# Loading the first layer's bias rows in the weight queue and transposing them by themselves

## The chip, the cores and the metric

The kernel runs on one core of a Trainium2 chip. Time is the device time of one execution in microseconds (us), and lower is better. A core has a matrix engine (PE; its weight loads are shown as PEld), a vector engine (DVE), an activation engine (ACT), a general engine (POOL) and a queue engine (SP) that only issues transfers. Each engine runs its own instructions in a fixed order and waits on semaphores for the others. Transfers between main memory and the on-chip memory run on 16 DMA engines, and they are issued from the instruction streams of SP, ACT and POOL.

## The reference

The input `x` has 2048 positions of 640 values. Two branches are computed from it and mixed by a gate per position:

```python
g = sigmoid((x * gate_w).sum(-1))                      # one gate per position
# branch a: a diagonal state space layer with 640 complex states
Lam_bar = exp(exp(log_dt) * Lam);  B_bar = ((Lam_bar - 1) / Lam)[:, None] * Bmat
h[t] = Lam_bar * h[t-1] + B_bar @ x[t]
a = 2 * real(h @ Cmat.T) + x * Dskip
# branch b: two dense layers, 640 -> 1728 -> 640
b = gelu(x @ w1 + b1) @ w2 + b2
out = g * a + (1 - g) * b
```

The change concerns `b1`, the 1728 biases of the first dense layer. The activation engine needs them as columns (one value per partition), and main memory holds them in one row.

## The kernel before, in words

The positions are worked on in four blocks of 512 (`q`), and within them in 16 chunks of 128 (`c`). For each block PE computes the first dense layer (`m1`: 14 column tiles `jf` of 128, the last one 64 wide, each a sum over five contraction slices `k` of 128) and the projection into the states (`bproj`). ACT applies the GELU with the bias column (`ge`) or copies the projection out (`u`). DVE runs the state recurrence (`pre`, `scan`, `post`, two halves of 256 positions per block) and leaves the states in `H`. For each chunk PE then computes the second dense layer (`m2`, L776 and L777) and the projection out of the states (`cproj`, L802, which reads the transposed matrix `CT`). DVE adds the parts up and SP stores them.

The order of the work is made by a planner when the kernel is built (`Sched.order`). Every operation is declared with its engine, an estimated duration, a latency after it, the keys that it reads and writes, and a priority (a smaller number goes first). The planner always takes the engine that is free earliest and gives it, among the operations whose inputs are there by the estimates, the one of smallest priority. The result is a fixed order for each engine. The chip keeps that order, whatever the real times are.

Dependencies follow the order of declaration (`Prog.op`). An operation that writes a key waits for the last writer that was declared before it and for all readers of that writer's data. PSUM banks are such keys, `("bank", n)`.

The start of the kernel is what the change touches. These are its parts, with the lines of the profile:

- **SP** issues, by priority: the first half of x's first block (`x0_0`, 0), the W1 slices for the first six column tiles (`w1_0` 2, `w1_1` 3), the second half (`x0_1`, 3.5), `w1_2` 4, `w1_3` 5, `w1_4` 6, the rest of W1 (`w1_r`, 6.5), then DMA transposes of B, of x's second block, W2, the transposes of the rest of x, and at last the ten transposes that make `CT` (all issues L330, the transposing ones L337).
- **ACT** issues six small loads into one tile `rows`: five rows each for the real part, the imaginary part and the step of the states, 13 rows of `b1`, and the last 64 values of `b1` twice, into both halves of the last row. Then it loads its first function table.
- **PE** transposes the first half of x (`tp0..`, L426), and starts the first layer of block 0 slice by slice over six banks (`m1_first`, L637). The slices are taken as (0, first half of the positions), (1, first), (2, first), (0, second), (1, second), (2, second), and then slices 3 and 4 over all 512 positions. The second half of x is transposed in between: `tp1` for k = 0, 1, 2 in bank 6 (six transposes) and for k = 3, 4 in bank 7 (four transposes).
- **The columns**: one transpose on PE (`cols`, L400, priority 6.2) turns all 29 rows into columns in bank 7. DVE copies them out (`cols1`, L405) to `cols`, of which `lcol` is the part of the states and `b1col` the part of the biases.
- **DVE** copies the transposes of x to `xT` (`tpe..`, L435) and computes tables from `lcol`: `ang` (L461, L462), `psi0`, `psi1`, `psi2` (L476 to L490), `atab` (L579 and L581), then `small` and the large tables. By priority the copies of x go before all of them, and `atab` (-946) comes after `psi0` to `psi2` (-949) and after `small` (-948) where these can run.
- **Bank 7** is used in the order of declaration: `cols`, `cols1`, then `tp1` for k = 3, 4 and its copy `tpe13`, and later a bank of `m1`.

Of the kernel before, what the change touches and what calls it, by code (L numbers as in the profile page):

```python
# [8 lines left out]
FP32 = mybir.dt.float32  # L9
BF16 = mybir.dt.bfloat16  # L10
# [137 lines left out]
class Prog:  # L148
# [8 lines left out]
    def op(self, name, eng, dur, reads, writes, fn, prio=None, lat=0.0, after=()):  # L157
        deps = {}
        for k in reads:
            for w in self.last_w.get(k, ()):  # L160
                deps[w.idx] = w
        for k in writes:
            for w in self.last_w.get(k, ()):
                deps[w.idx] = w
            for r in self.last_r.get(k, ()):
                deps[r.idx] = r
        for a in after:
            deps[a.idx] = a
        deps = list(deps.values())
        E = self.E  # L170

        def run(eg, deps=deps, eng=eng, fn=fn):
            E.wait(eng, *[d.done for d in deps])
            return fn()

        it = self.sch.add(name, eng, dur, deps, run, prio=prio, lat=lat)
        for k in writes:
            self.last_w[k] = [it]
            self.last_r[k] = []
        for k in reads:  # L180
            self.last_r.setdefault(k, []).append(it)
        return it


def bass_gated_mix__ssm_conv_s5__dense_activation_gelu__prompt_kernel(
# [20 lines left out]
    F = B_w1.shape[1]  # L206
    assert S % 512 == 0 and D % 128 == 0 and P == D
    KD = D // 128
    KP = P // 128
# [4 lines left out]
    NF = (F + 127) // 128  # L214
    FL = F - (NF - 1) * 128
# [10 lines left out]
    with ExitStack() as es, nc.Block() as block:  # L226

        def SB(name, shape, dt):
            return es.enter_context(nc.sbuf_tensor(name, list(shape), dt))
# [8 lines left out]
        GlL = [SB(f"GlL_{i}", [65, 512], BF16) for i in range(3)]  # L238
        dsk = SB("dsk", [128, D], BF16)
        gwb = SB("gwb", [128, D], BF16)  # L240
        NR = 3 * KP + NF
        rows = SB("rows", [NR, 128], BF16)
        cols = SB("cols", [128, NR], FP32)
        lcol = cols[:, 0:3 * KP].rearrange("p (a k) -> p a k", a=3)
        b1col = cols[:, 3 * KP:NR]
        dtb = SB("dtb", [128, KP], BF16)
        acol = SB("acol", [128, KP], FP32)
        thcol = SB("thcol", [128, KP], FP32)
# [5 lines left out]
        ident = SB("ident", [128, 128], BF16)  # L254
# [51 lines left out]
        op = pr.op  # L306

        def inc(eng, ins):
            return E.inc(eng, ins, eng + "_s")

        def dma_inc(eng, ins, sem):
            SEM(sem)
            E.count.setdefault(sem, 0)
            ins.then_inc(sems[sem], 16)
            E.count[sem] += 16
            return (sem, E.count[sem])
# [11 lines left out]
        def load(name, eng, sem, dst, src, writes, prio, dur=0.5, lat=2.5, reads=(), **kw):  # L328
            def fn():
                return dma_inc(eng, engines[eng].dma_start(dst, src), sem)  # L330
            return op(name, eng, dur, reads, writes, fn, prio=prio, lat=lat)
# [17 lines left out]
        NW = 6  # L349
# [5 lines left out]
        nmain = (NF - 1) * 128  # L355

        for i, (nm, src) in enumerate((("lre", A_Lambda_re), ("lim", A_Lambda_im), ("ldt", A_log_dt))):
            load(nm, "act", "l_" + nm, rows[i * KP:(i + 1) * KP, :], src.rearrange("(k p) -> k p", p=128), [("rows", i)], prio=-100 + i, dur=0.45)
        load("b1a", "act", "l_b1a", rows[3 * KP:NR - 1, :], B_b1[0:nmain].rearrange("(j p) -> j p", p=128), ["b1a"], prio=-97, dur=0.4, lat=2.5)
        for h in range(2):  # L360
            load(f"b1b{h}", "act", f"l_b1b{h}", rows[NR - 1:NR, h * 64:h * 64 + FL], B_b1[nmain:F].rearrange("(j p) -> j p", j=1), [("b1b", h)],
                 prio=-96 + h, dur=0.4, lat=2.5)


        def f_iota():
# [31 lines left out]
        psC = PS[7][:, :].bitcast(BF16)  # L397

        def f_cols():
            return inc("pe", nc.tensor.transpose(psC[:, 0:NR], rows[:, :], ident[0:NR, 0:NR]))  # L400

        op("cols", "pe", 0.2, [("rows", 0), ("rows", 1), ("rows", 2), "b1a", ("b1b", 0), ("b1b", 1), "ident"], [("bank", 7)], f_cols, prio=NW + 0.2)

        def f_cols1():
            return inc("dve", nc.vector.tensor_copy(out=cols[:, :], in_=psC[:, 0:NR]))  # L405

        op("cols1", "dve", 0.2, [("bank", 7)], ["lcol", "b1col"], f_cols1, prio=-3000)


        def filler(name, n, prio, deps):  # L410
# [552 lines left out]
```

## Time and profile before

| | us |
|---|---|
| median of 6 runs (range) | 217.96 (217.69 to 218.3) |
| the profiled execution | 217.87 |
| its span, first to last instruction | 216.0 |
| PE busy | 211.9 (98%) |
| DVE busy | 191.8 (89%) |
| ACT busy | 99.5 (46%) |
| DMA engines' mean share, 5.5 to 11 us | 1.01 |
| granted PE clock in the whole span | 1.00 |

The span is what the profile shows from the first to the last instruction. The time of the same execution is 1.87 us longer. An engine's idle time before an instruction is written in brackets behind the instruction with what ended it; "SPq" and "ACTq" are instructions by which an engine issues a transfer. A matmul's bar includes its way through the array, so bars of consecutive matmuls overlap, and the distance from start to start says what each costs.

### The profile page before, as it was taken

To read this page: it belongs to the slowest core of one execution; us is meant where nothing else is said; L and a number is where in the kernel's file an instruction comes from. 1 tells how busy PE (TensorE), PEld (TensorE's weight loads), DVE (VectorE), ACT (ScalarE), POOL (GpSimd) and SP (SyncE) were. 2 spreads that over 40 slices of the span, in tenths; PEclk is the share of its full clock that TensorE was granted. 3 is DMA by queue.
4 is the path that set the end of the run, shared out by engine and by line. 5 is a ranking of instruction groups with operands and counts; after the bars stand their busy time and mean duration, and the time that the engine had idled before them with its cause. 6 is when DMAs were issued, how large, how long until landed. Compare 5 with 4: busy or idle time off the path is not lost.

```text
span 216.0 us, 3326 instructions
## 1 busy us (share of the span) xinstructions
PE 211.9 (98%) x1305; PEld 124.9 (58%) x1305; DVE 191.8 (89%) x269; ACT 99.5 (46%) x169; POOL 4.6 (2%) x13
## 2 busy tenths in 40 slices
PE   8999999999999999999999999999999999999995
PEld 3744444444567776444457777544447777777774
DVE  5699999999999999999996999599999999989513
ACT  2497556675433324556662322556662224233220
POOL 1010030000000100000000010000000000000000
PEclk9999999999999999999999999999999999999999
DMA  6995569997810040000000014000000001000001
GB/s 164 356 161 108 121 151 287 281 183 130 129 37 30 30 155 0 30 0 0 3 0 0 33 35 148 33 0 0 0 3 0 0 30 33 30 30 33 30 30 33
DMA packets 28202, 15.46 MB, mean 72 GB/s; under 512 B 22044, under 2 KB 27740, under 8 KB 28188
## 3 DMA queue, kind: packets, MB, share of 16 engines
q1 hardware_dynamic: 27568, 12.95, 25.6%
q0 software_dynamic: 560, 2.30, 3.6%
q8 instruction: 11, 0.18, 0.3%
q14 instruction: 3, 0.02, 0.0%
q10 hardware_dynamic: 60, 0.01, 0.0%
HBM read 7.38 MB, written 2.62 MB: 46 GB/s over the span
## 4 chain that ended last, share of the span: by engine, by line
PE 70%; SPq 26%; DMA 1%; issue 1%; DVE 0%
PE ps L776 25%; SPq L337 24%; PE ps L802 20%; PE ps L656 13%; PE ps L701 10%; SPq L330 2%; PE ps L777 2%; DMA CT<-in_A_C_im_dram 1%; PE ps L677 1%; DVE osb L835 0%
## 5 line engine op out<-in xcount | busy, mean ns | idle before, releaser
L776 PE MATMUL ps<-W2sb,Gl 128*128 128x320 bf16 x416 | 61.4, 299 | 0.0
L656 PE MATMUL ps<-xT,W1sb 128*128 128x512 bf16 x230 | 50.3, 379 | 0.0
L776 PEld LDWEIGHTS ps<-W2sb,Gl 128*128 128x128 bf16 x416 | 40.5, 98 | 16.6 <-issue 0.4
L802 PE MATMUL ps<-CT,H 128*128 128x320 bf16 (+2 forms) x330 | 46.1, 295 | 0.4 <-DMA CT<-in_A_C_im_dram 0.4
L741 DVE TENSOR_TENSOR_SCAN W<-atab,V 128x1280 bf16<-128x1280 f32 x16 | 44.3, 2812 | 0.3
L701 PE MATMUL ps<-xT,BT 128*128 128x512 bf16 x200 | 43.8, 379 | 0.0
L664 ACT ACTIVATE Gl<-ps,cols 128x512 bf16<-128x512 f32 x46 | 31.4, 690 | 16.7 <-PE ps L656 16.6
L802 PEld LDWEIGHTS ps<-CT,H 128*128 128x128 bf16 x330 | 31.7, 98 | 12.6 <-DMA CT<-in_A_C_im_dram 0.7
L656 PEld LDWEIGHTS ps<-xT,W1sb 128*128 128x128 bf16 x230 | 22.5, 98 | 27.2
L784 ACT ACTIVATE E<-ps,g1col 128x320 bf16<-128x320 f32 x32 | 16.9, 527 | 43.1 <-PE ps L777 43.1
L701 PEld LDWEIGHTS ps<-xT,BT 128*128 128x128 bf16 x200 | 19.5, 98 | 23.5 <-issue 0.4
L710 ACT ACTIVATE U<-ps 128x512 bf16<-128x512 f32 x40 | 23.9, 597 | 18.3 <-PE ps L701 18.3
L813 ACT ACTIVATE E<-ps,gcol 128x320 bf16<-128x320 f32 x30 | 15.8, 527 | 25.4 <-PE ps L802 25.4
L502 DVE TENSOR_TENSOR osb<-xg,E 128x640 bf16<-128x640 bf16 x15 | 7.3, 487 | 8.5 <-ACT E L813 7.4
L821 DVE SCALAR_TENSOR_TENSOR xg<-xn,gcol,dsk 128x640 bf16<-128x640 bf16 x16 | 13.9, 883 | 0.4
L613 DVE SCALAR_TENSOR_TENSOR scr<-xn,gwb 128x640 bf16<-128x640 bf16 x16 | 13.2, 822 | 0.4
L502 DVE TENSOR_TENSOR H<-H,V 128x1280 bf16<-128x1280 bf16 x16 | 12.5, 822 | 0.3
L502 DVE TENSOR_TENSOR V<-V,W 128x1280 bf16<-128x1280 bf16 x16 | 12.5, 822 | 0.3
L502 DVE TENSOR_TENSOR V<-mr,U 128x2560 bf16<-128x2560 bf16 x8 | 11.9, 1489 | 0.5 <-DVE s L502 0.3
L502 DVE TENSOR_TENSOR H<-c,W 128x2560 bf16<-128x2560 bf16 x8 | 11.9, 1488 | 0.1
L502 DVE TENSOR_TENSOR V<-s,W 128x2560 bf16<-128x2560 bf16 x8 | 11.9, 1485 | 0.0
L502 DVE TENSOR_TENSOR W<-mi,U 128x2560 bf16<-128x2560 bf16 x8 | 11.9, 1484 | 0.0
(83 smaller groups left out, 100.6 us busy)
## 6 DMA issues: line engine op xcount, KB each, us to landing
out_dram<-osb SPq DMA_DIRECT2D x15, 160.0 KB, 1.8
W2sb<-in_B_w_dram SPq DMA_DIRECT2D x1, 2080.0 KB, 13.0
xn<-in_A_x_dram POOLq DMA_DIRECT2D x3, 640.0 KB, 4.7
W1sb<-in_B_w_dram SPq DMA_DIRECT2D x1, 1200.0 KB, 8.3
W1sb<-in_B_w_dram SPq DMA_DIRECT2D x5, 192.0 KB, 4.7
xn<-in_A_x_dram SPq DMA_DIRECT2D x2, 320.0 KB, 3.9
xT<-in_A_x_dram SPq DMA_TRANSPOSE x10, 3.7
dsk<-in_A_Dskip_dram POOLq DMA_DIRECT2D x1, 160.0 KB, 7.1
```

Source lines behind the costliest of these rows:

```text
L337: t = dma_inc("sp", nc.sync.dma_start_transpose(dst, src), sem)
L502: return inc("dve", nc.vector.tensor_tensor(out=o, in0=a, in1=b, op=o_))
L656: t = nc.tensor.matmul(PS[bank][:, :], W1sb[:, k, jf * 128:(jf + 1) * 128], xT[:, k, q * 512:(q + 1) * 512], start=(k == 0), stop=(k == KD ...
L664: return inc("act", nc.scalar.activation(Gl[q % 2][:, jf, :], PS[bank][:, :], ACT.Gelu_apprx_tanh, bias=b1col[:, jf:jf + 1]))
L701: t = nc.tensor.matmul(PS[bank][:, :], BT[:, kd, ci, k * 128:(k + 1) * 128], xT[:, kd, q * 512:(q + 1) * 512], start=(kd == 0), stop=(kd = ...
L710: return inc("act", nc.scalar.activation(dst, src, ACT.Copy, scale=1.0 if ci == 0 else -1.0))
L741: t = inc("dve", nc.vector.tensor_tensor_scan(out=g[:, ci, :], data0=a, data1=v[:, ci, :], initial=0.0, op0=ALU.mult, op1=ALU.add))
L776: t = nc.tensor.matmul(PS[bank][:, 0:HALF], Gl[q % 2][:, jf, ts], W2sb[:, jf, cols], start=(jf == 0), stop=False)
L784: return inc("act", nc.scalar.activation(E1[c % NE][:, cols], PS[bank][:, 0:HALF], ACT.Copy, scale=g1col[:, c:c + 1]))
L802: t = nc.tensor.matmul(PS[bank][:, 0:n], H[b % NHB][:, ci, k, s * 128:(s + 1) * 128], CT[:, k, ci, cols], start=(i == 0), stop=(i == 2 * K ...
L813: return inc("act", nc.scalar.activation(E2[c % NE][:, cols], PS[bank][:, 0:HALF], ACT.Copy, scale=gcol[:, c:c + 1]))
L821: return inc("dve", nc.vector.scalar_tensor_tensor(out=xg[c % 2][:, :], in0=xn[q % 2][:, c % 4, :], scalar=gcol[:, c:c + 1], in1=dsk[:, :] ...
```

## The change

The two tiles are parted: `rows` and `cols` keep only the 15 rows of the states, and the 14 bias rows get a tile `b1rows` and a column tile `b1col` of their own. Their loads leave ACT and go to SP with priorities 6.2 and 6.3, behind `w1_4` and in front of `w1_r`. The two loads of the last 64 values become one, whose source is read twice. The transpose `cols` stays at its priority and now waits for the three state loads only. A new transpose `colb` (priority 39.5) and its copy `colb1` (priority -1000) make the bias columns. They use bank 7, and they are declared directly behind `cols1`, in front of the transposes of x.

```diff
-        NR = 3 * KP + NF
-        rows = SB("rows", [NR, 128], BF16)
-        cols = SB("cols", [128, NR], FP32)
-        b1col = cols[:, 3 * KP:NR]
+        rows = SB("rows", [3 * KP, 128], BF16)
+        b1rows = SB("b1rows", [NF, 128], BF16)
+        cols = SB("cols", [128, 3 * KP], FP32)
+        b1col = SB("b1col", [128, NF], FP32)
...
-        load("b1a", "act", "l_b1a", rows[3 * KP:NR - 1, :], B_b1[0:nmain].rearrange("(j p) -> j p", p=128), ["b1a"], prio=-97, dur=0.4, lat=2.5)
-        for h in range(2):
-            load(f"b1b{h}", "act", f"l_b1b{h}", rows[NR - 1:NR, h * 64:h * 64 + FL], B_b1[nmain:F].rearrange("(j p) -> j p", j=1), [("b1b", h)],
-                 prio=-96 + h, dur=0.4, lat=2.5)
+        load("b1a", "sp", "l_b1a", b1rows[0:NF - 1, :], B_b1[0:nmain].rearrange("(j p) -> j p", p=128), ["b1a"], prio=6.2, dur=0.3, lat=2.5)
+        load("b1b", "sp", "l_b1b", b1rows[NF - 1:NF, :].rearrange("j (h p) -> j h p", h=2),
+             B_b1[nmain:F].rearrange("(j h p) -> j h p", j=1, h=1).broadcast_to([1, 2, FL]), ["b1b"], prio=6.3, dur=0.3, lat=2.5)
...
         def f_cols():
-            return inc("pe", nc.tensor.transpose(psC[:, 0:NR], rows[:, :], ident[0:NR, 0:NR]))
+            return inc("pe", nc.tensor.transpose(psC[:, 0:3 * KP], rows[:, :], ident[0:3 * KP, 0:3 * KP]))
...
-        op("cols", "pe", 0.2, [("rows", 0), ("rows", 1), ("rows", 2), "b1a", ("b1b", 0), ("b1b", 1), "ident"], [("bank", 7)], f_cols, prio=NW + 0.2)
+        op("cols", "pe", 0.2, [("rows", 0), ("rows", 1), ("rows", 2), "ident"], [("bank", 7)], f_cols, prio=NW + 0.2)
...
-        op("cols1", "dve", 0.2, [("bank", 7)], ["lcol", "b1col"], f_cols1, prio=-3000)
+        op("cols1", "dve", 0.2, [("bank", 7)], ["lcol"], f_cols1, prio=-3000)
+
+        def f_colb():
+            return inc("pe", nc.tensor.transpose(psC[:, 0:NF], b1rows[:, :], ident[0:NF, 0:NF]))
+
+        op("colb", "pe", 0.1, ["b1a", "b1b", "ident"], [("bank", 7)], f_colb, prio=6 * NW + 3.5)
+
+        def f_colb1():
+            return inc("dve", nc.vector.tensor_copy(out=b1col[:, :], in_=psC[:, 0:NF]))
+
+        op("colb1", "dve", 0.2, [("bank", 7)], ["b1col"], f_colb1, prio=-1000)
```

`KP` and `KD` are 5, `NF` is 14, `NW` is 6 and `FL` is 64.

More of the change, by code (lines that the diff above doesn't have):

```diff
@@ L240, in bass_gated_mix__ssm_conv_s5__dense_activation_gelu__prompt_kernel @@
         gwb = SB("gwb", [128, D], BF16)
-        NR = 3 * KP + NF
-        rows = SB("rows", [NR, 128], BF16)
-        cols = SB("cols", [128, NR], FP32)
-        lcol = cols[:, 0:3 * KP].rearrange("p (a k) -> p a k", a=3)
-        b1col = cols[:, 3 * KP:NR]
+        rows = SB("rows", [3 * KP, 128], BF16)
+        b1rows = SB("b1rows", [NF, 128], BF16)
+        cols = SB("cols", [128, 3 * KP], FP32)
+        lcol = cols[:, :].rearrange("p (a k) -> p a k", a=3)
+        b1col = SB("b1col", [128, NF], FP32)
         dtb = SB("dtb", [128, KP], BF16)
@@ L399, in f_cols @@
         def f_cols():
-            return inc("pe", nc.tensor.transpose(psC[:, 0:NR], rows[:, :], ident[0:NR, 0:NR]))
-        op("cols", "pe", 0.2, [("rows", 0), ("rows", 1), ("rows", 2), "b1a", ("b1b", 0), ("b1b", 1), "ident"], [("bank", 7)], f_cols, prio=NW + 0.2)
+            return inc("pe", nc.tensor.transpose(psC[:, 0:3 * KP], rows[:, :], ident[0:3 * KP, 0:3 * KP]))
+        op("cols", "pe", 0.2, [("rows", 0), ("rows", 1), ("rows", 2), "ident"], [("bank", 7)], f_cols, prio=NW + 0.2)
         def f_cols1():
-            return inc("dve", nc.vector.tensor_copy(out=cols[:, :], in_=psC[:, 0:NR]))
-        op("cols1", "dve", 0.2, [("bank", 7)], ["lcol", "b1col"], f_cols1, prio=-3000)
+            return inc("dve", nc.vector.tensor_copy(out=cols[:, :], in_=psC[:, 0:3 * KP]))
+        op("cols1", "dve", 0.2, [("bank", 7)], ["lcol"], f_cols1, prio=-3000)
[5 more added lines that the diff above has]
+        op("colb1", "dve", 0.2, [("bank", 7)], ["b1col"], f_colb1, prio=-1000)
         def filler(name, n, prio, deps):
```

## The prediction

> **What bounds the kernel now.** I read the page first, then the waits of PE, then the chain that ended last, and at last the first 13 us in order of time, engine by engine. The page:
>
> ```profile
> span 216.0 us, 3326 instructions
> ...
> PE 211.9 (98%) x1305; PEld 124.9 (58%) x1305; DVE 191.8 (89%) x269; ACT 99.5 (46%) x169; POOL 4.6 (2%) x13
> ```
>
> PE is the bound: 216.0 - 211.9 = 4.1 us of the span are all that it is not busy. The waits of PE say where, as the sum, the times and the longest:
>
> ```profile
> PE ps L385 <- PEq L948: 0.8, 1, 0.8
> PE ps L637 <- DMA W1sb<-in_B_w_dram: 0.4, 1, 0.4
> PE ps L802 <- DMA CT<-in_A_C_im_dram: 0.4, 1, 0.4
> ```
>
> Besides the start there are two gaps: at 5.6 us for a slice of W1, and at 61.3 us for the last transpose of CT. The rest is the tail behind PE's last matmul. The chain (start, length, what) shows what this makes of a delay at the start:
>
> ```profile
> 6.10 3.58 SPq L337
> ...
> 58.49 3.20 DMA CT<-in_A_C_im_dram
> 61.69 0.05 issue
> 61.74 2.89 PE ps L802 x20
> ```
>
> Up to 61.7 us the chain is SP's queue, which issues one transfer after another until CT is there; from then on it is PE without a gap. So two things can move the end: a later landing of CT, one for one, and a later PE, after the first 0.40 us, because PE would have stood 0.40 us at 61.3 anyway. An earlier DVE or ACT moves nothing. DVE's states are ready in time: the last H is written at 200.9 and read at 204.1 us.
>
> The change lies in the first 13 us. PE there:
>
> ```profile
> 4.88 0.73 PE L637 MATMUL ps<-xT,W1sb 128*128 128x256 bf16 x5
> 6.04 0.83 PE L637 MATMUL ps<-xT,W1sb 128*128 128x256 bf16 x6 [0.43 <-DMA W1sb<-in_B_w_dram]
> 6.80 0.18 PE L400 MATMUL ps<-ident,rows 29*128 29x29 bf16 x1
> 6.91 0.28 PE L637 MATMUL ps<-xT,W1sb 128*128 128x256 bf16 x1
> 7.03 0.72 PE L426 MATMUL ps<-ident,xn 128*128 128x128 bf16 x10
> 7.59 5.46 PE L637 MATMUL ps<-xT,W1sb 128*128 128x256 bf16 x36
> ```
>
> The columns are transposed at 6.80, then come all ten transposes of the second half of x, then 24 matmuls of 256 columns and 12 of 512 without a stop. The whole slices start 12 x 0.2155 = 2.59 us before the next group (12.89), at 10.30 us. DVE there:
>
> ```profile
> 7.02 0.19 DVE L405 CAST cols<-ps 128x29 f32<-128x29 bf16 x1 [1.62 <-PE ps L400]
> ...
> 7.76 0.95 DVE L435 COPY xT<-ps 128x256 bf16<-128x256 bf16 x3
> 8.63 0.32 DVE L476 TENSOR_TENSOR tr<-thcol,st_f 128x165 f32<-128x165 f32 x1
> ...
> 10.08 1.48 DVE L579 COPY atab<-amag 128x1280 f32<-128x1280 f32 x1
> ```
>
> **The order that the planner will make.** I work it by hand from the estimates in the code; it gives places in queues, no times. In the old order PE is free at 4.42 planned while the last bias row comes at 5.05, so `cols` falls behind six matmuls of slice 1, as seen. Now its rows are there at 3.85, and it is taken at 4.42, behind the first five matmuls. The decisive point is bank 7. `colb` and `colb1` are declared in front of `tp1` for k = 3, 4, so these four transposes wait for `colb1`, though their priority (12.4) is far smaller than that of `colb` (39.5). The rows of `colb` are there at 6.6 planned; at that time PE has 18 matmuls of priority 19 to 36 with all inputs, so `colb` is taken behind them (8.44). It doesn't come into the middle of slice 3, because slice 3 needs `tp1`'s k = 3. So PE's order becomes: `colb`, wait for `colb1` on DVE, four transposes, wait for their copy `tpe13` on DVE, slice 3. Nothing else is ready to fill in. On DVE `psi0` moves in front of the copies of x (acol is ready before), and at 7.78 planned only `atab` is ready, so it goes in front of `colb1` (8.54).
>
> **Cost, step by step.**
>
> *Loads off ACT.* Three issues (0.32, 0.27, 0.27) leave ACT at 2.0 to 2.9 us, and its function table can load earlier. ACT next worked at 7.24, waiting for the columns: worth 0.
>
> *cols earlier.* The state rows had landed at 2.10, 3.82 and 4.32 us (the trace's semaphore records), so `cols` runs in PE's 0.43 gap at 5.44. PE still waits for W1's second slice (landed 5.99) and x's second half (6.96), so the 0.3 us that `cols` took is not won in full. Six transposes from 7.03 end before W1's third slice lands (7.43), so slice 2 starts at 7.46 instead of 7.59: 0.13 won. The 18 + 6 matmuls then end at 10.30 - 0.13 = 10.17.
>
> *colb.* Transpose to end of DVE's copy took 7.21 - 6.80 = 0.41 with `cols`. With PE at 10.17 the copy could start at 10.39. DVE: the last of the six transposes ends at 7.53, so the copies start at 7.57. From the first copy to `atab` it was 10.08 - 7.76 = 2.32; without `psi0` (0.64) and the third copy (0.33) it is 1.35, so `atab` starts at 8.92. `atab` and its small memset took 1.6 (10.08 to 11.69), overlapping a little with what follows, so `colb1` starts at about 10.50 and ends at 10.69. PE and DVE meet almost at the same time; the queue on DVE adds only 0.1.
>
> *The rest of the round trip.* Four transposes took 0.39 to their end, the copy 0.42, and each crossing between engines 0.03 to 0.04: 10.69 + 0.03 + 0.39 + 0.04 + 0.42 + 0.03 = 11.60. Slice 3 starts there instead of 10.30: **PE is late by 1.3 us**. Bounds: without DVE's queue 1.2; with every crossing at 0.1 and `atab` late by 0.2, 1.75. I take 1.3, since every term has a row in this stage.
>
> *What is behind it.* All later PE work shifts by 1.3. Its inputs come no later than needed: `w1_r` landed at 12.50 and is needed at 14.2; ACT's first GELU had waited for a function table until 12.09 and now waits for bank 0 at 13.3, each 0.7 us against 1.08 us of PE; the states' U is complete at 32.0 + 1.3 = 33.3, before DVE takes it up at 34.25. On DVE, `small` started at 11.61 and now starts behind `tpe13` at about 11.6: the head start of the tables is used up, and nothing moves.
>
> *Two issues more on SP.* W1's issues took 0.43, the small ones on ACT 0.27 to 0.32, with 0.04 between: `w1_r` and all behind it are issued 0.62 to 0.95 later. The next issues were held: two transposes of B took 3.58 and 2.58 instead of 1.27, while the DMA engines were full (share 1.01 from 5.5 to 11 us). The data of `w1_r` began to move only when W1's slices were through (8.38), 4 us after its issue. So I take 0 for CT, and 0.95 as the upper bound. The bias rows queue behind `w1_4` and should land at 8.4 to 9.0, before 10.17.
>
> The DMA: Bandwidth & Descriptors page of the Trainium skill (Rules for kernel authors) says that issuing from several engines doesn't add bandwidth and only saves issue time on the sequencer. This speaks against moving loads onto SP, whose issues are the chain up to 61.7 us; by the rule alone the sum would be +0.95. The held issues say that this stretch of SP waits for data instead.
>
> **The sum.** The end moves by the larger of 1.3 - 0.40 = +0.9 (PE) and 0 to 0.95 (CT). Both agree within 0.05, so the size hardly depends on SP. Against the profiled execution (217.87) this is 218.77; the median shown (217.96) is 0.09 above that execution, so I say 218.87.
>
> On the clock: it was granted at 1.00 through the gap of 0.43 at 5.6, and the new gaps are about 0.4 and 0.5 (the four transposes lie between them). The page TensorE: Matmul & The Clock Gate (Part 1: The HAM clock gate) puts the return to half speed at an idle window of about 3.4 us, which these gaps don't reach; no run here shows such a drop in mid-kernel.
>
> **Rivals.**
>
> - *No stall on PE* (0.06): an input that I take as ready isn't, and `colb` falls into a gap of the plan before slice 2 ends. Its trip to DVE would be covered by matmuls, and only 0.1 us of transpose is added, less than the 0.40. With CT unmoved: 217.96, same. Against it: I find no gap in the plan. It decides if slice 3 starts before 10.7.
> - *SP's shift arrives in full, without the PE stall* (0.03): CT lands 0.62 to 0.95 later, PE is 0 to 0.1 late: 218.6 to 218.9. It needs every SP issue from B to CT to move by the same amount. Against it: the held issues.
> - *The bias rows land late* (0.05): small rows that share the queue's backlog complete only with `w1_r`, at 12.5. Then `colb` starts at 12.5, slice 3 at 12.5 + 0.41 + 0.93 = 13.84, PE is 3.5 late: +3.1, 221.1. For it: the 13 bias rows of 256 bytes took 3.4 us on ACT's queue from issue to landing (1.98 to 5.38). Against it: they stand in front of `w1_r`, and W1's slices landed one after another in their order of issue.
> - *Faster* (0.03): the end hangs on CT alone, and CT comes earlier. At most the 0.40 of PE's wait is to be had: 217.6. It needs the held issue on SP to end earlier with two small transfers in front, and it decides only if PE's first whole slice is no later than 10.3. I see nothing that speaks for it.
>
> My forecast has 0.83, with a range of its own of 218.6 to 219.4 (1.2 to 1.75 less 0.40, and 0.1 for the run). The range asked for is 218.3 to 219.5: it holds the forecast and the second rival. A change under 0.2% (0.44 us) can't be told from none; slower has 0.83 + 0.03 + 0.05 = 0.91, same 0.06, faster 0.03.
>
> **What would show it.** Right: L400's successor for the columns before 6.0 us, a second transpose at about 10.2, PE idle twice behind it with DVE as the releaser (about 0.4 and 0.5), the four transposes at 10.7, slice 3 at 11.6; PE's wait for CT at 61.3 gone; DVE's `atab` at 8.9 and directly behind it a copy of 14 columns. Wrong: slice 3 at 10.3 or earlier, `colb` waiting for a DMA, a wait for CT that is as long as before, or a clock below 1.00 after 11 us.

## The result and the profile after

The changed kernel takes 219.1 us (median of 23 runs, 218.42 to 219.79), the kernel before 218.05 (49 runs, 217.13 to 219.04). The ratio is 1.0049 with an interval of 1.0038 to 1.0059: about 1.05 us slower. The profiled execution took 219.14 us with a span of 217.3.

The waits of PE in the changed kernel (sum, times, longest):

```profile
PE ps L384 <- PEq L958: 0.8, 1, 0.8
PE ps L647 <- DVE xT L445: 0.5, 1, 0.5
PE ps L436 <- DVE b1col L414: 0.4, 1, 0.4
```

The wait for CT is gone, and in its place stand two waits for DVE. They lie at the start, as PE's order in time shows:

```profile
5.43 1.27 PE L647 MATMUL ps<-xT,W1sb 128*128 128x256 bf16 x5
6.64 0.18 PE L399 MATMUL ps<-ident,rows 15*128 15x15 bf16 x1
6.75 0.94 PE L647 MATMUL ps<-xT,W1sb 128*128 128x256 bf16 x7
7.52 0.50 PE L436 MATMUL ps<-ident,xn 128*128 128x128 bf16 x6
7.86 2.88 PE L647 MATMUL ps<-xT,W1sb 128*128 128x256 bf16 x24
10.67 0.18 PE L409 MATMUL ps<-ident,b1rows 14*128 14x14 bf16 x1
11.28 0.38 PE L436 MATMUL ps<-ident,xn 128*128 128x128 bf16 x4 [0.43 <-DVE b1col L414]
12.18 2.12 PE L647 MATMUL ps<-xT,W1sb 128*128 128x512 bf16 x9 [0.52 <-DVE xT L445]
```

The columns of the states are now transposed behind the first five matmuls, and six of the ten transposes of x follow. Behind the 24 matmuls stand `colb` (L409), a wait, the other four transposes, a wait, and slice 3 at 12.18 instead of 10.30. The chain that ended last goes through this place:

```profile
9.53 1.40 DVE atab L589
10.92 0.05 issue
10.97 0.17 DVE b1col L414
11.14 0.14 issue
11.28 0.40 PE ps L436 x4
11.67 0.02 issue
11.70 0.44 DVE xT L445
12.13 0.05 issue
12.18 2.76 PE ps L647 x12
```

From there on it is PE alone; SP's queue, which had carried the chain up to 61.7 us, is no longer on it. CT landed at 62.18 and PE took it up at 63.07, later by itself. SP's queue in the changed kernel, for the comparison with 4.18 (issue of W1's rest) and 46.66 (first issue of CT) before:

```profile
4.16 1.18 SPq L330 DMA_DIRECT2D b1rows<-in_B_b_dram  x2
5.39 0.41 SPq L330 DMA_DIRECT2D W1sb<-in_B_w_dram  x1
46.90 1.27 SPq L337 DMA_TRANSPOSE CT<-in_A_C_re_dram  x1
```

### The profile page after: what moved, and what is told of

Same layout as the page of the kernel before. It is cut to its first block, busy times and chain, and to the rows that moved or that the text cites. A ratio compares the mean times of both kernels' runs of the same rounds, so it can differ in the third digit from the quotient of the medians.

```text
span 217.3 us, 3330 instructions
## 1 busy us (share of the span) xinstructions
PE 213.1 (98%) x1306; PEld 125.7 (58%) x1306; DVE 191.5 (88%) x270; ACT 99.5 (46%) x169; POOL 4.6 (2%) x13
## 4 chain that ended last, share of the span: by engine, by line
PE 96%; DVE 2%; issue 0%; ACT 0%
PE ps L786 26%; PE ps L666 23%; PE ps L812 20%; PE ps L711 20%; PE ps L787 2%; PE ps L647 2%; PE ps L384 1%; PE ps L687 1%; PE ps L436 1%; DVE atab L589 1%; DVE xT L445 0%; PE ps L424 0%; DVE osb L845 0%; DVE tr L486 0%; DVE tr L500 0%
## 5 line engine op out<-in xcount | busy, mean ns | idle before, releaser
L674 ACT ACTIVATE Gl<-ps,b1col 128x512 bf16<-128x512 f32 x46 | 31.4, 690 | 16.8 <-PE ps L666 16.7
```

The lines of the kernel that those rows point to most:

```text
L674: return inc("act", nc.scalar.activation(Gl[q % 2][:, jf, :], PS[bank][:, :], ACT.Gelu_apprx_tanh, bias=b1col[:, jf:jf + 1]))
```

## The experiments

Three theories were set against each other: PE is late because four transposes of x wait for `colb1` (bank), SP's two more issues delay CT (queue), or PE's clock rises later (clock). The last came from the profile: the five matmuls at 5.43 us above took 1.27 where they had taken 0.73.

### Declared behind the transposes

```diff
-        op("colb", "pe", 0.1, ["b1a", "b1b", "ident"], [("bank", 7)], f_colb, prio=6 * NW + 3.5)
-        op("colb1", "dve", 0.2, [("bank", 7)], ["b1col"], f_colb1, prio=-1000)
...
         tpose_ev(1, 7, 0, (3, 4))
+        op("colb", "pe", 0.1, ["b1a", "b1b", "ident"], [("bank", 7)], f_colb, prio=6 * NW + 3.5)
+        op("colb1", "dve", 0.2, [("bank", 7)], ["b1col"], f_colb1, prio=-1000)
```

> The changed kernel with the declarations of colb and colb1 moved behind those of x's transposes and their copies; the loads stay on SP. Bank theory (PE is late because four transposes of x wait for colb1): the wait is gone, slice 3 follows the 24 matmuls directly, PE waits for CT again by 0.3 to 0.8 us, and the time is that of before within 0.4 us (217.7 to 218.4 against 218.05). Queue theory (two more issues on SP delay CT): the time stays 0.6 to 0.95 above before (218.7 to 219.0), with CT landing after 62.3 and PE waiting 1.0 us or more for it. Clock theory (PE's clock rises later in the changed kernel, which the profiled run shows at 6.6 us instead of 4.3): the late rise stays, and at least 0.5 us above before with it.

218.19 us (217.33 to 219.46, 12 runs) against 217.70 of before on the same chip, ratio 1.0030 (1.0010 to 1.0049). PE in order of time:

```profile
7.11 0.73 PE L425 MATMUL ps<-ident,xn 128*128 128x128 bf16 x10 [0.17 <-DMA xn<-in_A_x_dram]
7.68 3.52 PE L647 MATMUL ps<-xT,W1sb 128*128 128x256 bf16 x27
11.13 0.18 PE L452 MATMUL ps<-ident,b1rows 14*128 14x14 bf16 x1
11.24 2.12 PE L647 MATMUL ps<-xT,W1sb 128*128 128x512 bf16 x9
```

All ten transposes stand together again, 24 matmuls and the first three of slice 3 follow (the 27), then `colb` in the middle of slice 3, and nothing waits for it. The two waits for DVE are gone. In this execution (217.56 us) PE didn't wait for CT either, which the bank theory had wrong. But the median is 0.49 above before, just beyond the 0.4 that the bank theory allowed, and the runs spread over 2.1 us. Something beside the bank wait is there in some executions.

### The loads on ACT, the rest as changed

```diff
-        load("b1a", "sp", "l_b1a", b1rows[0:NF - 1, :], B_b1[0:nmain].rearrange("(j p) -> j p", p=128), ["b1a"], prio=6.2, dur=0.3, lat=2.5)
-        load("b1b", "sp", "l_b1b", b1rows[NF - 1:NF, :].rearrange("j (h p) -> j h p", h=2),
-            B_b1[nmain:F].rearrange("(j h p) -> j h p", j=1, h=1).broadcast_to([1, 2, FL]), ["b1b"], prio=6.3, dur=0.3, lat=2.5)
+        load("b1a", "act", "l_b1a", b1rows[0:NF - 1, :], B_b1[0:nmain].rearrange("(j p) -> j p", p=128), ["b1a"], prio=-97, dur=0.3, lat=2.5)
+        load("b1b", "act", "l_b1b", b1rows[NF - 1:NF, :].rearrange("j (h p) -> j h p", h=2),
+            B_b1[nmain:F].rearrange("(j h p) -> j h p", j=1, h=1).broadcast_to([1, 2, FL]), ["b1b"], prio=-96, dur=0.3, lat=2.5)
```

> The changed kernel with the two bias loads issued by ACT again, as before; the parted tiles, colb and its place stay. Bank theory: as slow as the changed kernel, 0.8 to 1.3 us above before (about 219.0), with slice 3 at 11.6 to 12.2. Queue theory: back to before within 0.4 us (218.05). If each has a part: 0.3 to 0.7 above before.

219.00 us (218.47 to 219.15, 5 runs) against 217.70, ratio 1.0061 (1.0049 to 1.0073):

```profile
7.63 2.88 PE L647 MATMUL ps<-xT,W1sb 128*128 128x256 bf16 x24
10.44 0.18 PE L409 MATMUL ps<-ident,b1rows 14*128 14x14 bf16 x1
11.05 0.38 PE L436 MATMUL ps<-ident,xn 128*128 128x128 bf16 x4 [0.43 <-DVE b1col L414]
11.95 2.76 PE L647 MATMUL ps<-xT,W1sb 128*128 128x512 bf16 x12 [0.52 <-DVE xT L445]
```

With SP's queue as it was, the loss is whole. The parted transpose with its place in bank 7 suffices for it, and the loads by SP aren't needed.

### CT in front, in both kernels

```diff
-               ["CT"], prio=10, dur=14.0)
+               ["CT"], prio=7.9, dur=14.0)
```

In the kernel before:

> The kernel before with CT's ten transposes issued in front of the last x transposes (priority 7.9 instead of 10). If PE's 0.40 us wait for CT is a limit of its own, as the prediction has it, CT lands by about 56, the wait at 61.3 is gone and the time falls by 0.3 to 0.5 us (217.55 to 217.75). If the end doesn't hang on CT, 218.05. If the earlier transposes crowd out something else, above 218.05.

217.28 us (11 runs) against 217.70, ratio 0.9984 (0.9970 to 0.9998). CT landed at 54.2 us, and PE doesn't wait for it. The gain, 0.42, is close to the 0.40 of the wait. This version is faster than both kernels, though its interval only just leaves 1.

In the changed kernel:

> The changed kernel with CT's transposes in front as well. Bank theory: PE comes to the first use of CT after CT has landed in any case, so nothing changes: 219.1 within 0.3 us, and the distance to the kernel before with the same edit is PE's whole delay, 1.3 to 1.6 us instead of 1.05. Queue theory: the time falls by 0.6 us or more (218.5 or less), since CT no longer sets the end.

218.80 us (218.60 to 219.01, 5 runs), with CT landing at 52.4. Against the kernel before on the same chip the ratio is 1.0058 (1.0046 to 1.0070), as without the edit (1.0049, and 1.0061 in the second experiment): the edit takes nothing off. The distance to the kernel before with the same edit, run on the same chip, is 1.52 us: PE's whole delay, when nothing of it is swallowed by the wait for CT. Without the edit the distance was 1.05, and 1.30 in the second experiment.

### The rest of the first experiment

Both edits together, `colb` declared behind the transposes and CT in front, loads on SP:

> colb behind x's transposes and CT's transposes in front: neither PE's wait for colb1 nor a late CT can set the end. The first of these edits alone left 0.5 us (1.003 of before) and a wide spread, 217.33 to 219.46. If that rest is CT, landing late in some executions because of the two more issues on SP, it goes here: 217.2 to 217.4, as the kernel before with CT in front (217.28), and the spread shrinks to 0.7. If the rest lies on PE's path at the start (colb itself, the parted columns), 0.3 to 0.6 above that: 217.6 to 217.9, with the spread kept.

217.49 us (217.11 to 217.76, 12 runs) against 217.53, ratio 0.9999 (0.9984 to 1.0014). Most of the spread is gone (0.65 us instead of 2.13), so that came through CT. The rest of 0.5 is gone only against the kernel before as it is. The kernel before with CT in front had been at 0.9984, and against that 0.0015, some 0.3 us, is left. The intervals overlap, so it isn't shown that this share lies on PE's path at the start, but nothing shows that it came through CT either; the time lies between the two ranges that I had given.

With CT in front on both sides, the place of the declarations alone is worth the step from 1.0058 to 0.9999 (each against before on its own chip), about 1.3 us. And the clock theory is answered: by the clock record PE's clock rose at 6.09 us in this execution, nearly as late as in the changed kernel (6.58), and the loss of 1.05 us is not there. At most the 0.3 us just named could be the clock's.

With the loads on ACT as well:

> Parted columns with the bias loads on ACT as before, colb behind x's transposes, CT's transposes in front. Nothing of the change that costs is left: bank theory and queue theory both say 217.0 to 217.4, at or up to 0.2 below the kernel before with CT in front (217.28), since the columns of the states come about 0.3 earlier on PE's path but colb adds 0.11.

217.75 us (217.47 to 217.99, 12 runs) against 217.53, ratio 1.0001 (0.9989 to 1.0014). That is above the range expected in us, and again 0.0017 above the kernel before with CT in front; the earlier start of the states' columns, which I counted as a gain of up to 0.2, brings nothing here either.

### Does SP's issue time reach CT?

The kernel before with the two loads by SP into a tile that nothing reads:

```diff
+        spare = SB("spare", [NF, 128], BF16)
...
+        load("b1x", "sp", "l_b1x", spare[0:NF - 1, :], B_b1[0:nmain].rearrange("(j p) -> j p", p=128), ["b1x"], prio=6.2, dur=0.3, lat=2.5)
+        load("b1y", "sp", "l_b1y", spare[NF - 1:NF, :].rearrange("j (h p) -> j h p", h=2),
+            B_b1[nmain:F].rearrange("(j h p) -> j h p", j=1, h=1).broadcast_to([1, 2, FL]), ["b1y"], prio=6.3, dur=0.3, lat=2.5)
...
+            for x in ("l_b1x", "l_b1y"):
+                nc.sync.wait_ge(sems[x], 16)
```

> The kernel before, with the two bias loads of the change issued by SP into a spare tile that nothing reads, in front of the rest of W1; all else as before. If the two issues cost time by themselves: 0.3 to 0.9 above before, with a wait of PE for CT of 0.7 to 1.3 instead of 0.4. If SP's held issues take them up, as the prediction has it: before within 0.2 us.

218.86 us (217.74 to 219.77, 8 runs) against 217.53, ratio 1.0058 (1.0036 to 1.0080): 1.33 us, more than either range allowed. The profiled execution waited for CT:

```profile
PE ps L806 <- DMA CT<-in_A_C_im_dram: 1.1, 1, 1.1
PE ps L660 <- DMA W1sb<-in_B_w_dram: 0.9, 1, 0.9
```

The second line is W1's rest; PE had come early to it, and the matmuls behind it started at 13.04, against 12.89 in the kernel before. The first line spoke for the queue. Four such loads (two tiles) were to give twice as much:

> The kernel before with four small bias loads (two of each) issued by SP into spare tiles that nothing reads, in front of the rest of W1: twice the two that cost 1.3 us. If SP's extra issues arrive at CT one for one, about 2.4 us of issues: 219.6 to 220.4, with PE waiting 2.0 to 3.0 us for CT. If they only reach CT beyond what the held issues take up, the step from two to four costs more than the first two. If they come through W1's rest landing late, PE waits 1.5 to 3 us at its first use near 13 us and CT's wait is short.

217.71 us (217.37 to 218.00, 10 runs) against 218.12, ratio 0.9991 (0.9976 to 1.0006): nothing. SP's queue shows why. In the kernel before (start, length, operation, number):

```profile
2.69 1.92 SPq L330 DMA_DIRECT2D W1sb<-in_B_w_dram  x4
4.66 10.27 SPq L337 DMA_TRANSPOSE BT<-in_A_B_re_dram  x5
46.66 1.27 SPq L337 DMA_TRANSPOSE CT<-in_A_C_re_dram  x1
```

And with the four loads:

```profile
4.19 2.18 SPq L331 DMA_DIRECT2D spare<-in_B_b_dram  x4
6.41 0.41 SPq L331 DMA_DIRECT2D W1sb<-in_B_w_dram  x1
6.86 7.55 SPq L338 DMA_TRANSPOSE BT<-in_A_B_re_dram  x5
46.73 1.27 SPq L338 DMA_TRANSPOSE CT<-in_A_C_re_dram  x1
```

The transposes of B begin 2.2 us later and take 2.7 less: the time in which they are held (an issue takes 1.27 us when it isn't) shrinks by what the issues before them took. CT's first issue stands at 46.73 instead of 46.66.

The control has the two loads into the spare tile issued by ACT, behind its six others:

> The control: the kernel before with the same two loads into a spare tile, but issued by ACT behind its six others. If the 1.3 us came from SP's issue time, nothing here: before within 0.2 us. If it came from the transfers themselves or from two more semaphores, 0.5 to 1.3 above before.

217.91 us (12 runs) against 218.12, ratio 0.9996 (0.9978 to 1.0014). Its profiled execution, with SP's queue as before, still had CT landing at 62.49, as late as with the two loads on SP (62.50).

The two loads by SP, with CT in front:

> The kernel before with the two loads by SP into a spare tile and CT's transposes in front of the last x transposes. If SP's two issues cost time through a late CT: the 1.3 us go, 217.2 to 217.5. If they cost it elsewhere (W1's rest, a semaphore at the end): 218.2 to 218.8.

217.58 us (12 runs) against 218.12, ratio 0.9984 (0.9970 to 0.9998): the same as without the loads. Whatever the two loads cost came through CT. And the two loads by SP a second time:

> The kernel before with two small bias loads issued by SP into a spare tile, a second time, because two cost 1.3 us and four cost nothing. If two issues on SP really delay CT: again 0.8 to 1.5 us above before and a wait for CT of 0.8 us or more. If what differed is when W2 and the transposes behind it get through (CT landed at 62.5 in that execution, and at 62.5 in one with no issue added on SP), it needn't come again: -0.3 to 0.7 against before.

217.99 us (217.44 to 219.86, 12 runs) against 217.75, ratio 1.0016 (0.9996 to 1.0036), with CT landing at 61.69 as in the kernel before, and a wait for it of 0.2. So the 1.3 us didn't come again. The same edit gave +1.33 and +0.24, and twice the edit gave -0.41. A shift of CT one for one with SP's issues is excluded by that. What stays open is when CT lands late: in the two profiled executions with CT at 62.5, W2 had landed at 44.06 and 43.82 instead of 41.96, and CT's first transpose was issued at 47.83 and 47.70 instead of 46.66. One of them had no issue added on SP. Over all profiled executions with CT's transposes in their old place, CT landed at 61.69, 62.12 and 62.49 in the three with no issue added on SP, and at 61.30 to 62.50 in the six with.

### The rows behind the rest of W1

```diff
-        load("b1a", "sp", "l_b1a", b1rows[0:NF - 1, :], B_b1[0:nmain].rearrange("(j p) -> j p", p=128), ["b1a"], prio=6.2, dur=0.3, lat=2.5)
-        load("b1b", "sp", "l_b1b", b1rows[NF - 1:NF, :].rearrange("j (h p) -> j h p", h=2),
-            B_b1[nmain:F].rearrange("(j h p) -> j h p", j=1, h=1).broadcast_to([1, 2, FL]), ["b1b"], prio=6.3, dur=0.3, lat=2.5)
+        load("b1a", "sp", "l_b1a", b1rows[0:NF - 1, :], B_b1[0:nmain].rearrange("(j p) -> j p", p=128), ["b1a"], prio=6.6, dur=0.3, lat=2.5)
+        load("b1b", "sp", "l_b1b", b1rows[NF - 1:NF, :].rearrange("j (h p) -> j h p", h=2),
+            B_b1[nmain:F].rearrange("(j h p) -> j h p", j=1, h=1).broadcast_to([1, 2, FL]), ["b1b"], prio=6.7, dur=0.3, lat=2.5)
```

> The changed kernel with the bias rows behind the rest of W1 instead of in front of it (priorities 6.6 and 6.7). If the rows land in the order of the queue, they come after W1's rest, at 11.7 to 12.6; colb waits for them on PE, slice 3 starts at 13.2 to 14.1 and the time is 1.2 to 2.0 above the changed kernel, 220.3 to 221.1. If small rows overtake it: 219.1.

222.49 us (221.18 to 222.59, 4 runs) against 217.53, ratio 1.0216 (1.0189 to 1.0242). PE:

```profile
12.86 0.16 PE L409 MATMUL ps<-ident,b1rows 14*128 14x14 bf16 x1 [2.23 <-DMA b1rows<-in_B_b_dram]
13.38 0.59 PE L436 MATMUL ps<-ident,xn 128*128 128x128 bf16 x4 [0.36 <-DVE b1col L414]
14.48 3.89 PE L647 MATMUL ps<-xT,W1sb 128*128 128x512 bf16 x12 [0.52 <-DVE xT L445]
18.21 4.05 PE L666 MATMUL ps<-xT,W1sb 128*128 128x512 bf16 x18
```

The rows land behind W1's rest (12.43 us, the rows 12.68 and 12.72), and `colb` waits 2.23 us for them. In the changed kernel they had landed at 7.49 and 8.18, before the last of W1's five slices (8.60) that was issued ahead of them. So the order of the queue isn't strict for them, but the 1200 KB of W1's rest they did not overtake. The wait explains 14.48 instead of 12.18 for slice 3. The rest is the clock, in the table of stretches (length, busy time of PE, PEld, DVE, ACT, POOL, granted clock, DMA share, GB/s):

```profile
12.80:14.40 1.60, 0.75 (x5) 0.44 (x5) 0.57 (x3) 1.09 (x1) 0.00 (x0) 0.68 1.02 206
14.40:16.40 2.00, 1.92 (x5) 0.73 (x6) 1.90 (x14) 0.20 (x1) 0.00 (x0) 0.50 0.53 108
16.40:18.00 1.60, 1.60 (x8) 0.65 (x7) 1.46 (x14) 0.67 (x2) 0.41 (x1) 0.88 0.61 136
18.00:20.00 2.00, 2.00 (x11) 0.94 (x10) 1.93 (x7) 2.00 (x5) 0.24 (x1) 1.00 0.79 133
```

It fell to half for 3.41 us (13.38 to 16.80 in the trace's clock record); the mean granted clock is 0.992 in each of the four runs. From the first of the 12 matmuls of the whole slices to the next group it is 18.21 - 14.48 = 3.73 us, against 14.78 - 12.18 = 2.60 in the changed kernel. My range, 220.3 to 221.1, had no term for these 1.1 us, and slice 3 came 0.4 us later than its end (14.1).

## Why the prediction was right

- **What bounds.** PE, and SP's queue up to CT: confirmed. CT in front took 0.42 off the kernel before, where the wait had been 0.40, and it took nothing off the changed kernel against before (1.0058 and 1.0049).
- **The order.** It came out as worked by hand: `cols` behind the first five matmuls, `colb` behind the 24, four transposes behind `colb1`, `psi0` in front of x's copies on DVE, `atab` in front of `colb1`. Moving only the declarations removed the two waits, and restoring only ACT's loads left them.
- **The round trip.** Expected 1.43 us from `colb` to slice 3 (10.17 to 11.60); measured 1.51, 1.51 and 1.50 in the three kernels that have it at full clock. The waits were to be 0.4 and 0.5; they are 0.43 and 0.52. DVE's queue adds 0.1 as said: `atab` ended at 10.92, PE's transpose at 10.85.
- **PE's delay.** Expected 1.3, measured 1.88 at slice 3 in the profiled pair, and 1.52 by the medians with CT in front, of which about 1.3 go with the declarations. The step that was mis-sized is the 0.13 won before slice 2: it was to start at 7.46 and started at 7.86, 7.63 and 7.51 in the three kernels, against 7.59 before. The sign that I gave for it, the states' columns before 6.0 us, did not come: `cols` was to fill a gap of PE at 5.44 and ran at 6.64, 6.42 and 6.29. There was no gap to fill. In these executions the five matmuls in front of `cols` started 0.21 us apart instead of 0.11 and the clock record begins at 6.58, 6.43 and 6.08, so PE ran at half clock until then (the mean granted clock of the span, 1.00, counts nothing ahead of the record). PE was late by itself: in the changed kernel x's second half landed at 7.19 and W1's third slice at 7.66, and PE came to the transposes at 7.52 and to slice 2 at 7.86. The 24 matmuls to `colb` took 2.81 instead of 2.71, the trip 0.08 more: 0.40 + 0.10 + 0.08 make the 0.58 between 1.3 and 1.88.
- **CT.** The shift of W1's rest was to be 0.62 to 0.95; it is 1.21 (issued at 5.39 instead of 4.18), as the second small load took 0.70 to issue. The 0 that I took for CT itself held on the whole: its first issue stands at 46.90 instead of 46.66. It landed 0.49 later (62.18), within the scatter of the executions. Four loads on SP confirm it. One reading behind the 0 was wrong: the data of W1's rest did not begin to move at 8.38, 4 us after its issue. Its first packets, of 1920 bytes each, moved at 7.06 by the trace's packets, while the last slices were still moving. What counts is that the rest landed at 11.70 instead of 12.50, though it was issued later. By the rule of the Trainium skill that I had set against the change (DMA: Bandwidth & Descriptors, Rules for kernel authors: several issuing engines save issue time) the two issues cost SP time. They did, 1.21 us, but it was taken out of a hold and didn't reach the end.
- **The sum.** 0.91 was expected, 1.05 is measured; the range and the sign hold. That the size came so close is in part luck, because both terms were too small. In the profiled pair PE is 1.88 late at slice 3 and 63.07 - 61.74 = 1.33 late at CT, so 0.55 was swallowed, not 0.40. The lines of the kernel before show why:

```profile
61.04 0.30 PE L777 MATMUL ps<-W2sb,GlL 65*128 65x320 bf16 x1
61.74 2.89 PE L802 MATMUL ps<-CT,H 128*128 128x320 bf16 x20 [0.40 <-DMA CT<-in_A_C_im_dram]
68.14 0.30 PE L777 MATMUL ps<-W2sb,GlL 65*128 65x320 bf16 x1
68.28 2.88 PE L802 MATMUL ps<-CT,H 128*128 128x320 bf16 x20
```

Where nothing waits, L802 starts 0.14 behind the matmul of L777; at 61.74 it started 0.70 behind it. From start to start the wait cost 0.56. The 0.40 in the brackets counts only from the end of L777's bar.

- **The rival of late rows** did not happen (`colb` waited for no transfer). Where it was forced, its price of 3.1 was too small: 4.96 was measured, with slice 3 at 14.48 instead of 13.84 and 1.1 for the clock.

## What to carry to other kernels

A priority can't lift an operation over a dependency that the order of declaration makes. Before two uses share a PSUM bank, look at which of them the planner must finish first, and what stands behind it. And where two chains meet at one point (here PE and CT at 61.7 us), ask for each what it costs with the other out of the way: delays in parallel don't add, and a gain in one of them is worth only its lead over the other.

## What the runs showed of the hardware that I had not expected

- PE's clock fell to half after an idle time of 2.23 us and another of 0.36 (the rows behind W1's rest), for 3.41 us. Gaps of 0.43 and 0.52 with four transposes between them left it at 1.00. The page TensorE: Matmul & The Clock Gate of the Trainium skill (Part 1: The HAM clock gate), which I drew on, puts the fall at an idle window of about 3.4 us; here it fell after less, 2.59 us of idle time in the 3.41 us ahead of the fall.
- The clock's first rise, by the trace's clock records, came at 3.7 to 5.9 us in six executions with the old start (4.34 in the profiled one of before) and at 5.2 to 6.6 in seven with the parted columns (6.58 in that of after). The first matmuls are the same in both. I don't know why. It doesn't explain the result: slice 2 started between 6.6 and 8.3 with the old start and between 7.5 and 7.9 with the parted columns, and the kernels with `colb` behind x's transposes rose late too (5.24 to 6.09) without the loss.
- The second small load (one row, its 64 values twice) took 0.70 us to issue on SP, more than W1's loads of 192 KB (0.43), and SP's held transposes made up for 2.2 us of issues in front of them.
